# A third buffer for queries, keys and weight pieces in the attention half of an attention and mixture kernel

## The chip, the cores and the metric

The kernel runs on one core of a Trainium2 chip. The metric is the device time of one execution in microseconds (us), lower is better.

## The reference

The first half is attention over 8 batches, 8 heads, 576 positions and 64 dimensions, with a bias from a small network over relative positions. The second half is a gated feed-forward product over 4608 tokens, 512 wide, with 1024 hidden features. Cut to what matters:

```
scores = q @ k.T / sqrt(64) + bias           # bias: relu(x @ w1 + b1) @ w2, per head
attn   = exp(scores - max); attn /= sum(attn) + 1e-9
x      = (attn @ v) as [4608, 512]
h      = (x @ moe_w1) * (x @ moe_w2) @ moe_w3
out    = h @ moe_w_out
```

The four weight matrices of the second half reach the kernel as 64-bit floats and are converted to 32 bits on the chip.

## The kernel before

Attention is cut into 32 units: 4 pairs of heads (p) times 8 batches (b), with u = 8p + b. A unit has nine score tiles of 128 rows: five from head 0 and the mixed tile, the rest from head 1. For each tile TensorE multiplies queries and keys into `s` (`op_S`, L322), VectorE adds the bias and takes the row minimum of the negated scores (`op_T`, L333), ScalarE takes the exponential into `pp` (`op_E`, L362), VectorE transposes it in blocks into `pt` (`op_R`, L372), and TensorE multiplies by the values into `acc` (`op_W`, L422). ScalarE copies `acc` to `x` (`op_X`, L431 and L436), which goes to DRAM (`op_x`, L442).

Loads (`op_l`, L305) are issued on SP's queue. Keys and queries come in halves: k0, q0, k1 and q1 of a unit are four tiles of the pool `raw`, which has two buffers of each, so unit u takes the buffers of unit u-2. Values land in the lower 64 partitions only, in five parts, and GpSimd copies each part to the upper 64 (`op_V`, L310). The bias of a pair of heads is read from DRAM (`load_bias`, L284 and L275), with a small memset on GpSimd ahead of each read.

A prologue computes the bias: VectorE and ScalarE make hidden values (L532, L530), TensorE multiplies them into `bacc` (L546), ScalarE copies that to `bev` (L552, L553; eight buffers), and SP writes 36 groups to DRAM as `nb_d` (L555).

In 24 of the units, six for each pair of heads, one piece of 128 x 512 weights is converted as well. `narrow` (L163) returns its nine steps: SP fetches the 64-bit piece as `wi` (`fetch`, L176), ScalarE makes `wmag` (L181), the lower bits (L185) and the sign (L188), and GpSimd clamps (L191), doubles three times (L211) and adds and multiplies up the result (L199, L201). `wi` and `wmag` are tiles of the pool `cva`, with two buffers. The last GpSimd step of a piece (L201) is the last reader of its `wi`. GpSimd carries these steps and the copies of values in one queue.

The order of work on TensorE, VectorE, ScalarE and GpSimd is written out by hand as times within a unit's period of 12.17 us, and each of the four engines keeps it. SP's queue has planned times too (`at["c0"] = 0.2, "SP"` is the fetch of a piece in its own unit), but its order is left to the planner, which may place an issue elsewhere. An issue in SP's queue waits for its buffer to be free and for its source, and whatever stands behind it in the queue waits too.

After attention, the second half folds moe_w3 and moe_w_out into one matrix (L665 to L678) and then runs 48 steps of products (L758, L772, L828). The pieces of moe_w1 and moe_w2 are fetched by the same `narrow` into `cva` (`fetch_w`, L600).

Of the kernel before, what the change touches and what calls it, by code (L numbers as in the profile page):

```python
# [17 lines left out]
P = 128  # L18
# [104 lines left out]
def relpos_attention_moe(  # L123
# [17 lines left out]
    nc = tc.nc  # L141
# [3 lines left out]
    NTOK, DO = out.shape  # L145
# [7 lines left out]
    def f(ap):  # L153
        return ap.bitcast(F32)
# [8 lines left out]
    def narrow(pool, src, n, x, queue, pieces=1, clamps=nc.vector, signed=False):  # L163

        d = {}

        def cut(ap):
            return ap if pieces == 1 else ap.rearrange("p (c n) -> p c n", c=pieces)

        def fetch():  # L170
            if not WIDE:
                queue.dma_start(cut(x), src)
                return
            wi = pool.tile([P, n, 2], I32, name="wi")
            flat = wi.rearrange("p n t -> p (n t)")
            queue.dma_start(cut(flat), src.bitcast(I32))  # L176
            mag = pool.tile([P, n], F32, name="wmag")
            d.update(lo=wi[:, :, 0], hi=wi[:, :, 1], mag=mag, bits=mag.bitcast(I32))

        def size():  # L180
            nc.scalar.activation(d["mag"], f(d["hi"]), AF.Abs)  # L181

        def rest():

            nc.scalar.activation(x, d["lo"].bitcast(U32), AF.Copy, scale=2.0 ** -51, bias=2.0)  # L185

        def sign():
            nc.scalar.activation(f(d["hi"]), f(d["hi"]), AF.Sign)  # L188

        def clamp():  # L190
            clamps.tensor_scalar(d["mag"], d["mag"], LEAST, MOST, op0=ALU.max, op1=ALU.min)  # L191

        def shift():

            nc.vector.tensor_scalar(d["bits"], d["bits"], 3, None, op0=ALU.logical_shift_left)

        def total():

            nc.gpsimd.tensor_tensor(x.bitcast(I32), x.bitcast(I32), d["bits"], op=ALU.add)  # L199
            if not signed:  # L200
                nc.gpsimd.tensor_tensor(x, x, f(d["hi"]), op=ALU.mult)  # L201

        def mark():

            nc.vector.scalar_tensor_tensor(
                x.bitcast(I32), d["hi"], -2 ** 31, x.bitcast(I32), op0=ALU.bitwise_and, op1=ALU.bitwise_xor,
            )

        def twice():

            nc.gpsimd.tensor_tensor(d["bits"], d["bits"], d["bits"], op=ALU.add)  # L211

        steps = [fetch, size, rest, sign, clamp, shift, total]
        if signed:
            steps = [fetch, size, rest, clamp, shift, mark, total]
        if clamps is nc.gpsimd:
            steps = steps[:5] + [twice] * 3 + [total]
        return steps if WIDE else [fetch] + [lambda: None] * (len(steps) - 1)
# [17 lines left out]
    w3s = [[held.tile([P, DO], F32, name=f"w3s{t}_{hf}") for hf in range(2)] for t in range(NF)]  # L236
    wos = [held.tile([P, DO], F32, name=f"wos{t}") for t in range(NF)]
    cva = ctx.enter_context(tc.tile_pool(name="cva", bufs=2))
# [9 lines left out]


    att, att_r = ctx.enter_context(ExitStack()), ctx.enter_context(ExitStack())  # L250
    raw = att_r.enter_context(tc.tile_pool(name="raw", bufs=2, side="right"))
    nbp = att_r.enter_context(tc.tile_pool(name="nbp", bufs=2, side="right"))
    vp = []
    units = [(p, b) for p in range(NPAIR) for b in range(B)]
    NU = len(units)
# [88 lines left out]
    for i in range(2):  # L344
        t = att.enter_context(tc.tile_pool(name=f"sums{i}", bufs=1)).tile([P, 64], F32, name=f"sums{i}")
# [97 lines left out]


    def piece_of(i):
        if i < NF:
            return narrow(cva, moe_w_out[i * P:(i + 1) * P, :], DO, wos[i], nc.sync, clamps=nc.gpsimd)
        hf, t = divmod(i - NF, NF)
        return narrow(cva, moe_w3[t * P:(t + 1) * P, hf * DO:(hf + 1) * DO], DO, w3s[t][hf], nc.sync, clamps=nc.gpsimd)

    pieces = dict(zip([u for u in range(NU) if 0 < u % B < B - 1], (piece_of(i) for i in range(3 * NF))))
    assert len(pieces) == 3 * NF

# [397 lines left out]
    for i in range(2 * NF):  # L851
        hf, t = divmod(i, NF)
# [31 lines left out]
    for n in range(NPR * NF):  # L884
# [28 lines left out]
        elif 0 < p < NPR - 1 and ft in (2, 5):  # L913
            i = int(ft > 4)
# [87 lines left out]
```

## Time and profile before

| what | value |
|---|---|
| median of three runs | 1075.87 us (1073.96 to 1077.92) |
| profiled execution, span of the trace | 1078.7 us |
| TensorE matmul busy | 1044.3 us, 97% |
| VectorE busy | 778.6 us, 72% |
| ScalarE busy | 558.4 us, 52% |
| GpSimd busy | 319.4 us, 30% |
| moved by DMA | 218.36 MB, mean 202 GB/s |

The profile gives no time for its execution other than the span of the trace, which stands 0.26% above the median of the runs. TensorE's busy time counts overlapping matmuls and is not a measure of how fully it is used. VectorE's work lies mostly in the first 455 us.

### The profile page before, as it was taken

Reading aid. Unit: us, or ns where it says so; the run is one execution under the profiler, and the core shown is the slowest. Engines: PE = TensorE matmul, PEld = TensorE weight load, DVE = VectorE, ACT = ScalarE, POOL = GpSimd, SP = SyncE. Lnnn points to the kernel's source line nnn. Section 1 sums busy time; section 2 is a strip of 40 time slices with the busy share of each in tenths; the row PEclk is TensorE's granted clock in tenths of the full one; section 3 lists DMA queues with packets and bytes.
Section 4 is the critical chain, followed back from the end, with each engine's and each line's share of the span. In section 5 each row is a group of like instructions: output and inputs, shape, how many; then the busy total and the mean of one; then the engine's idle time right before and its main releaser. Section 6 shows DMA issues by size and latency. Waiting matters only on the chain.

```text
span 1078.7 us, 33624 instructions
## 1 busy us (share of the span) xinstructions
PE 1044.3 (97%) x13968; PEld 830.1 (77%) x13968; DVE 778.6 (72%) x1486; ACT 558.4 (52%) x1269; POOL 319.4 (30%) x357
## 2 busy tenths in 40 slices
PE   7989999899989999999999999999999999999998
PEld 2346666566656666678899999999999999999997
DVE  8989999899989999998888455445635544453333
ACT  6958867776867787855454322323323232332222
POOL 0057756774767488674220000000000000000000
PEclk9979999999999999999999999999999999999999
DMA  8967676766576756356856766566475566556331
GB/s 260 299 187 220 197 224 205 215 205 192 168 218 188 211 172 188 122 151 233 276 215 216 264 215 227 189 235 223 167 251 206 183 226 223 189 185 215 140 134 59
DMA packets 93593, 218.36 MB, mean 202 GB/s; under 512 B 22016, under 2 KB 46720, under 8 KB 87296
## 3 DMA queue, kind: packets, MB, share of 16 engines
q1 hardware_dynamic: 93008, 216.19, 61.1%
q8 instruction: 110, 1.80, 0.7%
q14 instruction: 43, 0.35, 0.1%
q10 hardware_dynamic: 432, 0.02, 0.0%
HBM read 171.45 MB, written 44.71 MB: 200 GB/s over the span
## 4 chain that ended last, share of the span: by engine, by line
PE 80%; DVE 9%; issue 6%; DMA 2%; ACT 2%; POOL 1%; SPq 0%; DVEq 0%; ACTq 0%; POOLq 0%
PE X L758 16%; PE acc L422 13%; PE Y L758 12%; PE s L322 12%; PE oc L828 9%; PE od L828 9%; DVE ts L333 4%; PE bacc L546 3%; DVE pt L372 3%; PE X L772 3%; PE Y L772 3%; PE wacc L678 1%; POOL w3s L667 1%; DMA wi<-in_moe_w_dram 1%; DMA w1c<-in_w_dram 0%
## 5 line engine op out<-in xcount | busy, mean ns | idle before, releaser
L422 PE MATMUL acc<-pt,v 32*64 32x160 f32 (+1 forms) x9216 | 215.9, 297 | 10.4 <-issue 10.4
L422 PEld LDWEIGHTS acc<-pt,v 32*64 32x64 f32 x9216 | 161.7, 132 | 77.5 <-issue 50.7
L362 ACT ACTIVATE pp<-ts,mx 128x576 f32<-128x576 f32 x256 | 196.0, 766 | 39.9 <-DVE mx L333 39.1
L322 PE MATMUL s<-k,q 64*128 64x288 f32 (+1 forms) x1280 | 198.4, 450 | 7.0 <-DVE mx L333 6.3
L758 PE MATMUL X<-xS,wS 128*128 128x384 f32 x960 | 194.8, 338 | 0.0
L333 DVE CUSTOM_DVE_ANT_0 ts<-s,nb 128x576 f32<-128x576 f32 x256 | 183.1, 737 | 13.5 <-PE s L322 13.2
L758 PEld LDWEIGHTS X<-xS,wS 128*128 128x128 f32 x960 | 171.5, 188 | 6.8
L372 DVE STREAM_TRANSPOSE pt<-pp 128x1152 f32<-128x1152 f32 x128 | 175.2, 1370 | 2.0 <-ACT pp L362 1.7
L322 PEld LDWEIGHTS s<-k,q 64*128 64x128 f32 (+1 forms) x1280 | 92.3, 180 | 78.9 <-issue 35.7
L758 PE MATMUL Y<-xS,wS 128*128 128x384 f32 x720 | 145.1, 336 | 0.0
L801 DVE TENSOR_TENSOR wos<-X,wos 128x384 f32<-128x384 f32 x80 | 44.6, 557 | 138.8 <-PE X L758 138.8
L310 POOL COPY v<-v 64x512 f32<-64x512 f32 (+1 forms) x160 | 87.6, 564 | 154.3 <-DMA v<-in_v_dram 141.7
L758 PEld LDWEIGHTS Y<-xS,wS 128*128 128x128 f32 x720 | 127.9, 188 | 0.1
L805 ACT COPY wos<-X 128x384 f32<-128x384 f32 x80 | 38.3, 479 | 125.6 <-PE X L758 125.6
L781 ACT ACTIVATE ghd<-wos 128x384 fp32r<-128x384 f32 x48 | 25.2, 525 | 125.7 <-DVE wos L801 105.6
L828 PE MATMUL oc<-w3s,ghc 128*128 128x512 f32 x288 | 89.8, 393 | 0.0
L828 PE MATMUL od<-w3s,ghd 128*128 128x512 f32 x288 | 89.6, 392 | 0.0
L801 DVE TENSOR_TENSOR wos<-Y,wos 128x384 f32<-128x384 f32 x80 | 44.6, 557 | 49.9 <-ACT wos L805 36.4
L211 POOL TENSOR_TENSOR wmag<-wmag 128x512 int32<-128x512 int32 x72 | 74.7, 1038 | 5.9
L781 ACT ACTIVATE ghc<-wos 128x384 fp32r<-128x384 f32 x48 | 25.2, 526 | 93.8 <-DVE wos L801 76.2
L828 PEld LDWEIGHTS oc<-w3s,ghc 128*128 128x128 f32 x288 | 53.5, 188 | 8.6
L828 PEld LDWEIGHTS od<-w3s,ghd 128*128 128x128 f32 x288 | 53.5, 188 | 8.5
(97 smaller groups left out, 1401.5 us busy)
## 6 DMA issues: line engine op xcount, KB each, us to landing
wS<-w_d SPq DMA_DIRECT2D x40, 1792.0 KB, 7.4
q<-in_q_dram SPq DMA_DIRECT2D x64, 288.0 KB, 4.3
wi<-in_moe_w_dram SPq DMA_DIRECT2D x32, 512.0 KB, 3.9
w_d<-wS SPq DMA_DIRECT2D x8, 1792.0 KB, 6.6
v<-in_v_dram SPq DMA_DIRECT2D x96, 128.0 KB, 4.4
nb_d<-bev SPq DMA_DIRECT2D x36, 295.5 KB, 4.2
k<-in_k_dram SPq DMA_DIRECT2D x64, 144.0 KB, 4.4
nb<-nb_d SPq DMA_DIRECT2D x16, 576.0 KB, 5.5
```

What stands on the lines that cost most here:

```text
L211: nc.gpsimd.tensor_tensor(d["bits"], d["bits"], d["bits"], op=ALU.add)
L310: nc.gpsimd.tensor_copy(t[64:128], t[0:64])
L322: nc.tensor.matmul(s[outs, hf, :HS], d[f"q{h}"][rows, q0:q0 + n], d[f"k{h}"][rows, :], start=True, stop=True,)
L333: nc.vector.tensor_tensor_reduce(out=halves(ts), in0=d.pop(("s", t))[:, :, :HS], in1=halves(NB[p, t]), op0=ALU.add, op1=ALU.min, scale=-1. ...
L362: nc.scalar.activation(d["p", ps][:, k * S:(k + 1) * S], ts, AF.Exp, bias=mx, scale=-1.0, accum_out=SUMS[u // 4 % 2][:, col:col + 1],)
L372: nc.vector.transpose(o, st[u].pop(("p", ts)))
L422: nc.tensor.matmul(acc[outs, a, c0:c0 + 32 * (t1 - t0)], d["v", b][rows, h], pt_[rows, t0:t1, 32 * b:32 * b + 32], start=(b == 0), stop=(b ...
L758: nc.tensor.matmul(acc, w[:, l, W_AT[n], i * P:(i + 1) * P], x[:, r, X_AT[n]], start=(k in "125" and i == 0 and m == 0), stop=(i == 1 and ...
L772: nc.tensor.matmul(acc, w[:, l, i * P:(i + 1) * P], x[:, r, 2 * k + "cd".index(j)], start=(n == 0), stop=(n == 11),)
L781: nc.scalar.activation(st[n], st["g" + j], AF.Copy)
L801: nc.vector.tensor_tensor(st[o], x, y, op=op)
L828: nc.tensor.matmul(d["o", j, t], l[:, sl], folded[ft][r], start=(ft == 0 and n == 0), stop=(ft == NF - 1 and n == 2),)
```

## The change

The pool `raw` gets a third buffer of each of its four tiles, so a unit takes the buffers of the unit three before. A new pool `cvb` with one buffer holds `wi` and `wmag` of every third weight piece; the other two of three stay in `cva`. So a piece takes the buffers of the piece three before. No instruction is added or taken away, and the planned times stay. The new pool and the larger one lie in on-chip memory until the end of attention.

```
-    raw = att_r.enter_context(tc.tile_pool(name="raw", bufs=2, side="right"))
+    raw = att_r.enter_context(tc.tile_pool(name="raw", bufs=3, side="right"))
     nbp = att_r.enter_context(tc.tile_pool(name="nbp", bufs=2, side="right"))
+    cvb = att_r.enter_context(tc.tile_pool(name="cvb", bufs=1, side="right"))
...
     def piece_of(i):
+        cv = cvb if i % 3 == 2 else cva
         if i < NF:
-            return narrow(cva, moe_w_out[i * P:(i + 1) * P, :], DO, wos[i], nc.sync, clamps=nc.gpsimd)
+            return narrow(cv, moe_w_out[i * P:(i + 1) * P, :], DO, wos[i], nc.sync, clamps=nc.gpsimd)
         hf, t = divmod(i - NF, NF)
-        return narrow(cva, moe_w3[t * P:(t + 1) * P, hf * DO:(hf + 1) * DO], DO, w3s[t][hf], nc.sync, clamps=nc.gpsimd)
+        return narrow(cv, moe_w3[t * P:(t + 1) * P, hf * DO:(hf + 1) * DO], DO, w3s[t][hf], nc.sync, clamps=nc.gpsimd)
```

## Rows read from the trace of the kernel before

**Rows 1.** Windows: us, busy (x instructions) by engine, TensorE clock, DMA share, GB/s.
```profile
150.00:200.00 50.00, 49.55 (x1380) 32.09 (x1364) 49.53 (x98) 38.47 (x95) 30.71 (x41) 1.00 0.68 202
200.00:250.00 50.00, 45.72 (x1211) 29.96 (x1215) 45.22 (x89) 35.79 (x88) 38.99 (x45) 0.97 0.73 213
...
300.00:350.00 50.00, 45.46 (x1180) 29.69 (x1180) 43.76 (x86) 34.65 (x87) 34.14 (x41) 0.93 0.69 200
```

**Rows 2.** Timeline of TensorE in one stall: start, us, work, idle before.
```profile
320.11 0.69 PE L422 MATMUL acc<-pt,v 32*64 32x160 f32 x2 [3.11 <-issue]
```

**Rows 3.** Timeline of GpSimd around the same stall.
```profile
308.07 1.30 POOL L201 TENSOR_TENSOR w3s<-w3s,wi 128x512 f32<-128x512 f32 x1
...
318.88 0.60 POOL L310 COPY v<-v 64x512 f32<-64x512 f32 x1 [5.57 <-DMA v<-in_v_dram]
```

**Rows 4.** Timeline of SP's queue around the same stall.
```profile
309.39 0.33 SPq L176 DMA_DIRECT2D wi<-in_moe_w_dram  x1
...
314.20 0.51 SPq L305 DMA_DIRECT2D v<-in_v_dram  x1
```

**Rows 5.** Waits of SP's queue, 50 to 430 us: total, times, longest.
```profile
SPq L176 <- POOL w3s L201: 50.0, 12, 6.0
SPq L305 <- PE s L322: 33.6, 72, 1.6
```

**Rows 6.** Tile k: the matmuls' idle time by what ended it: us, times.
```profile
  DVE mx L333: 36.8, 91
  issue: 35.7, 132
```

**Rows 7.** Tile wi: its readers, and their idle time that its transfer ended.
```profile
L181 ACT ACTIVATE wmag<-wi x40: 643/670/688, 68.9 to 566.2; 128x512 f32<-128x512 f32 x40
...
  DMA wi<-in_moe_w_dram: 2.3, 2
```

**Rows 8.** Timeline of SP's queue in the prologue.
```profile
7.34 0.43 SPq L176 DMA_DIRECT2D wi<-in_moe_w_out_dram  x1
10.32 2.40 SPq L555 DMA_DIRECT2D nb_d<-bev  x2
12.77 0.59 SPq L176 DMA_DIRECT2D wi<-in_moe_w_out_dram  x1
```

**Rows 9.** DMA issues: KB each, median us from issue to landing.
```profile
q<-in_q_dram SPq DMA_DIRECT2D x64, 288.0 KB, 4.3
wi<-in_moe_w_dram SPq DMA_DIRECT2D x32, 512.0 KB, 3.9
...
k<-in_k_dram SPq DMA_DIRECT2D x64, 144.0 KB, 4.4
```

**Rows 10.** Windows of the prologue and behind it, columns as in rows 1.
```profile
0.00:5.00 5.00, 0.00 (x0) 0.00 (x0) 0.40 (x1) 1.28 (x1) 0.44 (x6) 1.00 0.56 156
0.00:20.00 20.00, 12.79 (x112) 5.55 (x112) 15.36 (x40) 11.68 (x24) 0.44 (x6) 1.00 0.80 252
20.00:50.00 30.00, 28.29 (x230) 8.78 (x226) 30.00 (x89) 28.14 (x64) 0.00 (x0) 1.00 0.94 303
60.00:65.00 5.00, 4.68 (x20) 1.95 (x20) 4.05 (x10) 3.36 (x8) 2.01 (x4) 0.50 0.50 141
```

**Rows 11.** Timeline of SP's queue where the bias is last written and read.
```profile
54.00 0.53 SPq L555 DMA_DIRECT2D nb_d<-bev  x1
...
60.46 0.45 SPq L275 DMA_DIRECT2D nbM<-nb_d  x1
```

**Rows 12.** Tile bev: issue to landing of its writes, min, median, max.
```profile
DMA to landing us min/median/max: 3.2/4.2/6.9
```

**Rows 13.** Timeline at the end of attention.
```profile
447.26 0.39 SPq L176 DMA_DIRECT2D wi<-in_moe_w_dram  x1
...
452.30 1.06 POOL L310 COPY v<-v 64x512 f32<-64x512 f32 x2 [3.40 <-DMA v<-in_v_dram]
...
453.00 2.48 PE L422 MATMUL acc<-pt,v 32*64 32x160 f32 x112
```

## The prediction

> **What bounds the kernel now.** I read the windows first, since the page's shares mix two halves with different limits. In an undisturbed stretch of attention VectorE is busy for 49.53 of 50 us, so there VectorE sets the pace. Two stretches fall short of it: 45.22 us in 200 to 250 and 43.76 in 300 to 350 [rows 1]. Taking the undisturbed stretch as the level, they lose 49.53 - 45.22 = 4.31 and 49.53 - 43.76 = 5.77 us, together 10.1 us. That is the prize in this part of the kernel, and whatever the new buffers may save has to be found there, at the start, or at the end of attention. The second half of the kernel touches none of the new tiles.
>
> The timelines show what such a stall is made of. TensorE stands idle 3.11 us before a value product at 320.11 [rows 2]. The product needed a part of the values that GpSimd had copied at 318.88, and GpSimd had stood idle 5.57 us for its transfer [rows 3]. That transfer was issued only at 314.20, in a queue where SP had been held until 309.39 by the fetch of a weight piece [rows 4]. The fetch waited for GpSimd's last step on an older piece, which ended at 308.07 + 1.30 = 309.37 [rows 3]. So a late GpSimd holds SP, SP sends the values late, and late values make GpSimd later. SP's waits on that step come to 50.0 us in 12 waits between 50 and 430 us, and its waits for the score product that frees keys and queries to 33.6 us in 72 [rows 5]. These waits are what the change is aimed at.
>
> The next question is whether the loads that get a third buffer are themselves ever late. They are not. The score products, which read keys and queries, stood idle chiefly for VectorE's row minimum (36.8 us, it frees the score buffers) and for issue (35.7 us), with no transfer of keys or queries at the head of the list [rows 6]. The readers of the weight pieces waited 2.3 us in all for the pieces' transfers [rows 7]. What is late is the values, and they get no new buffer.
>
> **The change part by part.**
>
> No instruction is added or removed on any engine, so no engine gets more or less work. What can change is when SP's issues go out.
>
> *Where the planner puts a load.* Here lies the choice on which the forecast rests. If SP kept its planned times, a fetch with three buffers would find its buffer free a period earlier, and the waits in rows 5 would go. But SP does not keep them. The fetches of pieces 0 and 1 are planned in units 1 and 2, behind every write of the bias, and they stand in the queue at 7.34 and at 12.77, among the first of those writes [rows 8], while the first reader of a piece runs at 68.9 [rows 7]. They are placed as soon as a buffer is free by the planner's reckoning, however early that is. The fetch at 309.39 is the same case: it is issued 0.02 us after the step that frees its buffer, and it stands ahead of value loads that are planned before it. With a third buffer the planner does the same with one buffer more. At the start it fills three sets instead of two. From then on, the load that stands behind the release of a given buffer is the one for the unit three ahead instead of two ahead, at the same place in the queue and with the same wait on the same instruction. The data come a period earlier, which no reader needed, and the values stand behind the same waits as before.
>
> *Weight pieces in the steady state.* The wait of each fetch on L201 stays, 50.0 us of SP's time in rows 5, and so do the two stalls: 0 us. From the other side, if all of those waits went and took the stalls along, 10.1 us would be gained.
>
> *Keys and queries in the steady state.* Same place, same wait for the score product: 0 us. They are covered by the distance between load and use, a whole unit; a loss would need them later than now, and nothing makes them later.
>
> *The start.* The third set is loaded in the prologue: two halves of keys, two of queries and a weight piece, 2 x 144 + 2 x 288 + 512 = 1376 KB, or 1.41 MB [rows 9]. At 303 GB/s, the rate of 20 to 50 us [rows 10], that is 4.65 us of transfer. It is free if it fits in the gaps. The DMA engines are busy 0.80 of the first 20 us and 0.94 of the next 30, which leaves 4.0 + 1.8 = 5.8 us; but 0.44 x 5 = 2.2 us of it lie in the first 5 us, before these loads can be sent, so 3.6 us are left [rows 10]. 4.65 - 3.6 = 1.05 us would still be ahead of the last bias data at 50 us. That matters there, because SP waits from 54.00 until 60.46 for the last bias write to land before it can read the mixed tile's bias, and loads of values stand behind that read [rows 11]. I take 1.0 us. The lower bound is 0 (the landing is hidden by the prologue's compute, in which VectorE is busy for all of 20 to 50 us) and the upper 4.65 (no gap can be used). The issues themselves, five at some 0.4 to 0.6 us as in rows 8, are covered by the eight buffers of `bev`: a write may be late until its buffer is wanted again eight groups on, the 36 writes go out from 10.32 to 54.00 [rows 8, 11], 1.25 us apart, so eight take 10 us, and the writes land in 4.2 us at the median and 6.9 at most [rows 12]. If that cover is gone, they cost up to 3 us, within the upper bound above.
>
> *The end.* The second half's first two fetches take buffers of `cva`. The last piece now sits in `cvb`, so they move up one place in the queue and one place falls empty: the one at 447.26, where a fetch holds SP until GpSimd is done with the last piece. The values behind it go earlier, and GpSimd's 3.40 us of idle time at 452.30 can shrink. TensorE takes up its value products at 453.00, before the second of those copies is done at 453.36 [rows 13], so these copies release nothing that TensorE was held for. I take 0; the bound is a gain of 3.4 us.
>
> The sum: +1.0 at the start, 0 in the steady state, 0 at the end. On the profiled execution 1078.7 + 1.0 = 1079.7 us; on the median of the runs, 2.8 us below it, 1075.87 + 1.0 = 1076.9 us. The bounds of these terms alone give 1075.9 - 3.4 = 1072.5 to 1075.9 + 4.65 = 1080.5.
>
> **The rivals.**
>
> *The waits go, and it is faster.* If the planner leaves the fetches near their planned places, or finds the free buffer but puts values ahead of them, SP is no longer held by GpSimd and the loop of lateness is broken. For it speaks that the stalls begin exactly there [rows 3, 4]; against it, the place of the fetches in rows 8 and of the one in rows 4. The time is 1075.9 - 10.1 = 1065.8 us if both stalls go, and 1075.9 - 5.8 = 1070.1 if one does. The Trainium skill (Perfetto Trace Analysis, Optimization Strategy) says that a gap which keeps coming back on the engine that ought to be saturated can mean that too few buffers are there for the next tile. By that rule the kernel would gain these 10.1 us; the trace agrees that a buffer's release is waited for, but shows the tile behind that wait, the values, to be another than the ones that get buffers.
>
> *The start is bound by its transfers, and it is slower.* If none of the 4.65 us fits in a gap, the last bias write lands so much later than 60.46, and the values behind it too. TensorE is already slowed then: from 60 to 65 us its granted clock is 0.50, the lower of its two levels, and VectorE is busy for 4.05 of 5 us [rows 10]. TensorE would stand idle longer before, and if the slow stretch grows by the same 4.65 us, VectorE loses another 0.95 / 5 of it, 0.9 us, up to all of it. That is 4.65 + 0.9 = 5.6 to 9.3 us, so 1081.5 to 1085.2. It decides from 5.4 us on. Against it stand the gaps in the shares, and that ScalarE and VectorE bound the prologue.
>
> *The change does nothing at all* is the forecast itself but for 1.0 us.
>
> **How the numbers follow.** About 0.5%, 5.4 us, is what a measurement of this kernel can tell from no change. The forecast, with the order of the queue moving up along with the buffers, gets 0.64, and all of its own range, 1072 to 1081, lies within 0.5%. The faster rival gets 0.18: rows 8 speak plainly, but only of the start. The slower one gets 0.18, less likely in its full size, but the only part of the sum that is sure to exist is at the start. So faster 0.18, same 0.64, slower 0.18. The range has to take in most of both rivals to leave out no more than 2 in 10: from 1066, where both stalls go, to 1083, the lower half of the slow case.
>
> **What would show it.** Right: three fetches of weight pieces and three sets of keys and queries in SP's queue before 30 us; SP's waits on L201 of the w3 pieces still near 50 us between 50 and 430; VectorE short of its pace again near 206 to 222 and 309 to 325 us; the first score tiles later by about 1 us. Wrong: the waits on L201 gone and no shortfall of VectorE in those windows (the first rival); the last bias write landing 4 us later or `bev` waiting for its buffers (the second). The forecast fails altogether if the planner's new order moves the value loads themselves, since one stall more or less is worth 4 to 6 us.

## The result: slower by 0.7%, lost at the hand-over from the bias to attention

The changed kernel takes 1083.38 us (median of 6 runs, 1078.79 to 1084.35) where the kernel before takes 1075.91 in the same session: ratio 1.0068, 95% interval [1.0042, 1.0094]. The forecast was 1076.9 with a range of 1066 to 1083, so the time lies just above the range, on the side that had a chance of 0.18.

The windows of the kernel after, first those that answer to [rows 1], with the same columns:

```profile
150.00:200.00 50.00, 48.94 (x1322) 31.77 (x1316) 49.02 (x96) 36.68 (x92) 31.17 (x39) 1.00 0.72 204
200.00:250.00 50.00, 46.89 (x1282) 30.69 (x1285) 47.31 (x94) 37.73 (x93) 36.19 (x42) 1.00 0.68 200
...
300.00:350.00 50.00, 47.26 (x1258) 30.68 (x1259) 46.87 (x94) 37.37 (x92) 36.51 (x43) 0.99 0.69 204
...
20.00:50.00 30.00, 28.30 (x230) 8.84 (x228) 30.00 (x89) 28.09 (x65) 0.00 (x0) 1.00 0.97 327
50.00:100.00 50.00, 39.45 (x739) 22.88 (x745) 38.37 (x75) 29.61 (x71) 22.11 (x27) 0.80 0.66 200
55.00:60.00 5.00, 0.13 (x2) 0.00 (x0) 0.00 (x0) 0.39 (x2) 0.00 (x0) 0.89 0.94 326
60.00:65.00 5.00, 2.29 (x8) 1.15 (x8) 4.40 (x7) 1.63 (x4) 2.62 (x5) 0.50 0.57 159
...
70.00:75.00 5.00, 3.99 (x18) 2.03 (x16) 4.95 (x9) 2.78 (x7) 0.00 (x0) 0.50 0.59 178
75.00:80.00 5.00, 5.00 (x80) 2.62 (x78) 3.17 (x6) 2.48 (x7) 3.76 (x4) 0.56 0.07 14
```

Of the kernel before, the same view of the stretches that the prediction had not shown:

```profile
50.00:100.00 50.00, 44.97 (x926) 26.59 (x928) 44.65 (x88) 35.57 (x85) 26.98 (x33) 0.86 0.67 201
...
70.00:75.00 5.00, 5.00 (x140) 3.20 (x124) 3.49 (x8) 2.47 (x7) 4.71 (x5) 0.69 0.30 87
75.00:80.00 5.00, 5.00 (x167) 3.29 (x157) 3.53 (x9) 3.68 (x9) 3.93 (x6) 1.00 0.58 173
```

From 55 to 60 us the computing engines all but stand still while the DMA engines are 0.94 busy. VectorE does 44.65 - 38.37 = 6.28 us less of its work between 50 and 100 us. After the pause TensorE's granted clock is 0.50, the lower of its two levels, up to 75 us and 0.56 up to 80; before it was 0.69 from 70 us and back at 1.00 from 75 us on. The prologue itself is not later: from 20 to 50 us the engines are as busy as in [rows 10], and only the transfers are more, 327 GB/s where there were 303. The two stalls of [rows 1] are still there, in other sizes.

What stands still is visible on VectorE. Its timeline after, and then before:

```profile
54.24 0.08 DVE L334 DVE_READ_ACCUMULATOR2_ANT mx<- 128x1 f32 x1
60.60 1.38 DVE L373 STREAM_TRANSPOSE pt<-pp 128x1152 f32<-128x1152 f32 x1 [6.28 <-DMA v<-in_v_dram]
```

```profile
54.34 1.37 DVE L372 STREAM_TRANSPOSE pt<-pp 128x1152 f32<-128x1152 f32 x1
```

The first transpose of attention starts at 60.60 instead of 54.34 and waits 6.28 us for a DMA. It reads and writes nothing that a transfer brings. The name in the brackets is only that of the transfer that landed last. SP's timeline after says which one it is:

```profile
53.90 0.53 SPq L557 DMA_DIRECT2D nb_d<-bev  x1
...
60.17 0.45 SPq L276 DMA_DIRECT2D nbM<-nb_d  x1
```

The last write of the bias is issued at 53.90 (before: 54.00 [rows 11]), and SP's read that needs all of them to have landed goes out at 60.17. The transpose follows 0.43 us later. Before, only SP waited for that landing, now VectorE does too, and with it TensorE:

```profile
62.69 2.29 PE L323 MATMUL s<-k,q 64*128 64x288 f32 x8 [7.56 <-DVE mx L334]
```

**Why it waits: where the tiles lie.** The bigger pools sit on the right side of on-chip memory, ahead of the prologue's pool of `bev`. A third set of keys and queries takes 2 x 1152 + 2 x 2304 = 6912 B in each partition (144 and 288 KB over 128 partitions, [rows 9]), a third `wi` and `wmag` 4096 + 2048 = 6144 B, together 13,056 B. That moves the eight `bev` buffers (2368 B each) down. In the memory map of the built kernel before they start 3040 B above the end of `pt`, the transposes' output. No trace shows that map, but the first experiment finds the border between 3040 and 3072 B. After the change 13,056 - 3040 = 10,016 B are common to both. So the first transpose may not write until the transfers out of `bev` are done.

The queue did what was forecast. SP's waits after, 50 to 430 us, which answer to [rows 5]:

```profile
SPq L176 <- POOL w3s L201: 45.4, 13, 6.1
...
SPq L306 <- PE s L323: 26.1, 46, 3.7
```

The fetches still wait for the same step, 45.4 us in 13 waits where there were 50.0 in 12, and the loads for the score products that free keys and queries, 26.1 us in 46 where there were 33.6 in 72. The profiled executions are closer than the medians: 1081.8 against 1078.7 us is +3.1. VectorE lost 6.28 us between 50 and 100 us, and between 100 and 450 us (sum of the seven windows) it did 339.99 us against 336.80, 3.19 more, because this execution's later stalls were smaller: 6.28 - 3.19 = 3.09. That the two figures meet so closely is chance. Between the medians lie 7.5 us. That the later stalls even out over many executions and only the start remains is a reading, since there is one trace of each kernel; the first experiment's 7.0 us agree with it.

### The profile page after: what moved, and what is told of

The parts are those of the page before. It is cut to its first block, busy times and chain, and to the rows that moved or that the text cites. A ratio compares the mean times of both kernels' runs of the same rounds, so it can differ in the third digit from the quotient of the medians.

```text
span 1081.8 us, 33616 instructions
## 1 busy us (share of the span) xinstructions
PE 1043.5 (96%) x13968; PEld 829.8 (77%) x13968; DVE 780.3 (72%) x1486; ACT 558.5 (52%) x1269; POOL 319.2 (30%) x357
## 4 chain that ended last, share of the span: by engine, by line
PE 83%; DVE 6%; issue 4%; DMA 2%; ACT 2%; POOL 2%; SPq 0%; DVEq 0%; ACTq 0%; POOLq 0%
PE X L760 16%; PE acc L423 15%; PE s L323 14%; PE Y L760 12%; PE oc L830 9%; PE od L830 9%; PE bacc L548 3%; PE X L774 3%; PE Y L774 3%; DVE ts L334 3%; DVE pt L373 2%; POOL w3s L669 1%; DMA wi<-in_moe_w_dram 1%; DMA v<-in_v_dram 0%; ACT bev L555 0%
```

## Experiments

The theory to test was memory (the place of `bev` against `pt`); its rivals were the extra loads in the prologue and the new order of the queue. Further down come the two later stalls, on which the prediction rested.

**A dead pool in the kernel before, 3040 B and 3072 B.** No load, buffer or queue changes, but for one small memset on GpSimd.

```
     nbp = att_r.enter_context(tc.tile_pool(name="nbp", bufs=2, side="right"))
+    gap = att_r.enter_context(tc.tile_pool(name="gap", bufs=1, side="right")).tile([P, 760], F32, name="gap")
+    nc.gpsimd.memset(gap[:, 0:8], 0.0)
```

The second has 768 columns in place of 760.

> The kernel before with 3040 bytes per partition of dead space between the bias tiles and the prologue's eight bev buffers, so that bev ends up exactly against pt without sharing a byte with it. It loads nothing more and has no third buffer. Memory theory (the larger pools push bev into the place of pt, and the first transpose waits for the last bias write to land): no shared byte, so no stall at the first transpose and a time within 2 us of before. Transfer theory (the third set's loads in the prologue delay it): no more loads, within 2 us of before too. It is the control of the next run.

> The same with 3072 bytes, 32 more, so that bev and pt share 32 bytes per partition. Still no third buffer and no more loads. Memory theory: the first transpose waits from about 54.4 until the last bias write lands at about 60.4 us, VectorE stands idle some 6 us there, and the run is 5 to 8 us slower than before (ratio 1.005 to 1.007). Transfer theory and queue theory (the third buffers change the order of SP's queue): as in the control, within 2 us of before.

Measured: 1075.74 us, ratio 1.0009 [0.9996, 1.0021], and 1082.78 us, ratio 1.0060 [1.0035, 1.0086]. VectorE's timeline with 3040 B and with 3072 B, and SP's with 3072 B:

```profile
54.40 1.37 DVE L374 STREAM_TRANSPOSE pt<-pp 128x1152 f32<-128x1152 f32 x1
```

```profile
59.76 1.38 DVE L374 STREAM_TRANSPOSE pt<-pp 128x1152 f32<-128x1152 f32 x1 [5.18 <-DMA v<-in_v_dram]
```

```profile
54.15 0.52 SPq L557 DMA_DIRECT2D nb_d<-bev  x1
...
59.70 0.45 SPq L277 DMA_DIRECT2D nbM<-nb_d  x1
```

32 B of unused memory cost 7.0 us between the two medians. The transpose starts 0.06 us after the read that waits for the last write. The loss of the change is there without any of its buffers or loads.

**The change, and the kernel before, with the two pools apart.** In both the pool `pt` is opened ahead of the values' pools, so that it lies elsewhere, and `bev` has seven buffers.

```
-        ep = pro.enter_context(tc.tile_pool(name="ep", bufs=8, side="right"))
+        ep = pro.enter_context(tc.tile_pool(name="ep", bufs=7, side="right"))
...
-    vp += [att.enter_context(tc.tile_pool(name=f"vp{i}", bufs=1)) for i in range(2)]
     pt = att.enter_context(tc.tile_pool(name="pt", bufs=1))
+    vp += [att.enter_context(tc.tile_pool(name=f"vp{i}", bufs=1)) for i in range(2)]
```

> The changed kernel with pt placed below the value pools instead of above them and seven bev buffers instead of eight, so that pt and bev share nothing (the second unit's values do). All third buffers and the loads of the third set in the prologue stay. Memory theory: no stall at the first transpose, and 5 to 8 us faster than the changed kernel, so within 3 us of before. Transfer theory: the extra 1.41 MB are still loaded, so it stays 5 to 8 us slower than before. Queue theory: the order of SP's queue is that of the changed kernel, so it stays slower too.

> The kernel before with the same two placements as the run with pt and bev apart (pt below the value pools, seven bev buffers), and two buffers as before. All theories: within 2 us of before. What the run with third buffers differs from this one by is the worth of the buffers and their loads: 0 to +1.5 us by the memory theory, 5 to 8 us by the transfer theory.

Measured: with third buffers 1073.36 us, ratio 0.9990 [0.9972, 1.0009]; with two, 1073.63, ratio 0.9990 [0.9975, 1.0005]. The first transpose of the one with third buffers:

```profile
54.25 1.37 DVE L373 STREAM_TRANSPOSE pt<-pp 128x1152 f32<-128x1152 f32 x1
```

The stall is gone with all the loads in place. What the third buffers do besides, in the queue, at the start and at the end, is the difference of these two: -0.3 us, nothing that can be told from zero with intervals of some 2 us to either side.

**One half of the change each.** First only `raw` with three buffers, then only `cvb` with `raw` at two.

```
-    raw = att_r.enter_context(tc.tile_pool(name="raw", bufs=2, side="right"))
+    raw = att_r.enter_context(tc.tile_pool(name="raw", bufs=3, side="right"))
```

> One half of the change: three buffers of keys and queries, weight pieces as before. The pool is 6912 bytes larger, so bev's first two buffers reach into pt. Memory theory: any shared byte brings the whole wait, so the first transpose starts at about 60 us and the run is 5 to 8 us slower than before, as with 32 shared bytes. A theory by amounts (the cost grows with the shared bytes or with the bytes loaded) would give about half, 3 to 4 us.

> The other half: every third weight piece in tiles of its own, two buffers of keys and queries. The pool of 6144 bytes also moves bev's first two buffers into pt. Memory theory: the same whole wait, 5 to 8 us slower than before. Theory by amounts: 3 to 4 us.

Measured: 1082.84 us, ratio 1.0070 [1.0043, 1.0097], and 1085.61 (4 runs), ratio 1.0097 [1.0069, 1.0124]. VectorE's timeline of the second:

```profile
60.45 1.38 DVE L373 STREAM_TRANSPOSE pt<-pp 128x1152 f32<-128x1152 f32 x1 [6.07 <-DMA nb_d<-bev]
```

6912 - 3040 = 3872 B and 6144 - 3040 = 3104 B in common are enough for all of the loss, as the 32 B were. The parts do not add up, the price is that of one wait. Here the wait is even named after the write of `bev`. The second costs 0.3% more than the whole change and more than the 5 to 8 us expected; the intervals overlap. Its trace has a stall that belongs to neither theory, TensorE waiting for queries:

```profile
245.20 1.33 PE L323 MATMUL s<-k,q 64*128 64x288 f32 x4 [2.60 <-DMA q<-in_q_dram]
```

Whether the other three executions have it too is open.

**SP freed from the fetches, then from every wait for GpSimd.** The prediction held that late GpSimd work keeps SP, and SP the values [rows 2 to 4]. First the pieces of attention are fetched from ScalarE's queue, in the kernel before and in the change with the pools apart; then the small memsets of `load_bias` move to VectorE as well.

```
-            return narrow(cva, moe_w_out[i * P:(i + 1) * P, :], DO, wos[i], nc.sync, clamps=nc.gpsimd)
+            return narrow(cva, moe_w_out[i * P:(i + 1) * P, :], DO, wos[i], nc.scalar, clamps=nc.gpsimd)
...
-            nc.gpsimd.memset(nb[:, 0, 0:1], 0.0)
+            nc.vector.memset(nb[:, 0, 0:1], 0.0)
```

> The kernel before, with the weight pieces of attention fetched from ScalarE's queue instead of SP's, so that the fetch stands at its planned place in ScalarE's order and SP never waits for GpSimd's last step on a piece. Two buffers as before, nothing moved in memory. Theory that SP is held by those fetches and so sends the values late: SP's waits on L201 in 50 to 430 us, 50 to 70 us in all, are gone, VectorE is busy for over 48 of 50 us in 200 to 250 and 300 to 350, and the run is 4 to 10 us faster than before (ratio 0.991 to 0.996). Rival (the values are held by the bias reads and their memset on GpSimd, or by GpSimd itself): within 2 us of before, and the two windows stay near 45 us.

> The same fetches from ScalarE's queue, in the changed kernel with pt and bev apart. The fetch now stands at a planned place and does not move up with the buffers, so the third buffer of the pieces is real slack. If the release of the piece's buffer is still waited for in ScalarE's queue with two buffers, this is faster than the run before it by up to 3 us; if not, the same within 1.5 us.

> The run with weight pieces fetched from ScalarE's queue, and in addition the 15 small memsets ahead of the bias reads on VectorE instead of GpSimd, so that SP's queue waits for GpSimd neither before a fetch nor before a bias read. Two buffers, memory as before. Theory that the values are late because SP is held by a late GpSimd, whichever instruction it waits on: the 63.9 us and 9.2 us of SP's waits on the memsets go too, VectorE is busy for over 48 of 50 us in 200 to 250 and 300 to 350, and it is 4 to 8 us faster than the run before it in this line (1076.9), less some 1.5 us of memsets on VectorE. Rival (GpSimd's own queue is what delays the copies of values: their conversions stand ahead of them, whenever SP sends them): within 2 us of that run, and the two windows stay below 47 us.

> The same with the third buffers of keys, queries and pieces, and with pt and bev apart. First theory: as the run above, or up to 2 us faster where a third buffer takes away a wait for a score product or for a piece's last step. Rival: within 2 us of the run with three buffers and ScalarE's queue (1076.6).

Measured, as ratios: fetches moved, 1.0020 [1.0008, 1.0033] (1076.86 us) and, with third buffers, 1.0005 [0.9982, 1.0028]; memsets moved too, 1.0009 [0.9988, 1.0031] (1074.84 us) and 0.9994 [0.9973, 1.0014]. SP's waits with the fetches moved, and with both moved and two buffers:

```profile
SPq L305 <- PE acc L422: 67.8, 74, 3.5
SPq L284 <- POOL nb L281: 63.9, 12, 8.3
```

```profile
SPq L305 <- PE acc L422: 130.6, 109, 4.2
...
SPq L284 <- DVE nb L281: 6.7, 7, 1.3
```

The windows of the last one:

```profile
200.00:250.00 50.00, 46.65 (x1213) 30.78 (x1206) 44.32 (x89) 35.22 (x86) 37.47 (x42) 0.93 0.66 201
300.00:350.00 50.00, 48.18 (x1310) 31.44 (x1308) 47.28 (x99) 37.93 (x94) 40.35 (x46) 0.97 0.69 213
```

With two buffers the waits on L201 are gone, then all longer waits for GpSimd, and VectorE still has 44.32 us in 200 to 250, less than the 45.22 of [rows 1]; in 300 to 350 it has 47.28, more than the 43.76 there. TensorE's longest gap in the first of these windows:

```profile
235.12 1.33 PE L422 MATMUL acc<-pt,v 32*64 32x128 f32 x20 [2.19 <-issue]
```

An SP that GpSimd holds is not what makes the stalls. SP still waits in these runs, now for TensorE (130.6 us), so that values could be late for another reason; the gaps themselves decide that.

**What TensorE waits for instead.** In the kernel before it has five gaps of more than 0.7 us in attention's steady state. They are put down to "issue", and they lie in the middle of a value product, which reads one `pt` and one part of the values: in three of them 62 or 63 of its 64 matmuls have already run, in the one of [rows 2] 46 of 48 and in the one at 236.20 us 44 of 64. No new value can be missing there. In 200 to 250 us they come to 1.41 + 2.01 + 0.86 = 4.28 us, where VectorE falls short by 4.31. Two of them, beside the one in [rows 2]:

```profile
215.16 0.43 PE L422 MATMUL acc<-pt,v 32*64 32x160 f32 x2 [2.01 <-issue]
...
307.73 0.29 PE L422 MATMUL acc<-pt,v 32*64 32x160 f32 x1 [0.99 <-issue]
```

Windows that run from the start into these three gaps count what TensorE has done by then:

```profile
0.00:214.50 214.50, 196.68 (x4282) 112.52 (x4283) 202.47 (x437) 163.73 (x388) 106.08 (x133) 0.97 0.75 226
0.00:307.30 307.30, 286.84 (x6703) 171.27 (x6704) 291.06 (x610) 232.58 (x558) 168.03 (x207) 0.97 0.73 217
...
0.00:318.50 318.50, 296.10 (x6958) 177.19 (x6959) 302.02 (x630) 239.56 (x574) 173.69 (x213) 0.97 0.73 216
```

6958 - 6703 = 255 matmuls, with their weight loads 510 instructions. The page of the profile lists a DMA queue of instructions:

```profile
q8 instruction: 110, 1.80, 0.7%
```

That is 110 packets of 16.4 KB. TensorE's 2 x 13,968 = 27,936 matmuls and loads and 185 semaphore and drain instructions of its sequencer, which the trace also holds, are 28,121, one packet for every 256 (28,121 / 256 = 109.8). Counted with the sequencer's, the five gaps begin after 8385, 8641, 9665, 13,505 and 14,017 instructions: 1, 4, 15 and 2 times 256 apart. In the other traces, too, every gap of over 0.7 us in the middle of a value product lies on this grid, to within one instruction. Theory A is that TensorE ran out of instructions. The DMA view of 316.0 to 317.4, and of 317.5 to 318.7, in the gap that ends at 320.11:

```profile
q1 hardware_dynamic: 363, 0.34, 94.8%
```

```profile
q1 hardware_dynamic: 129, 0.11, 33.1%
q8 instruction: 1, 0.02, 6.2%
```

Data take 94.8% of the 16 DMA engines until 317.4. The instruction packet runs only after that, and TensorE goes on 1.4 us behind its end. In all five gaps the packet before it ends 1.3 to 1.5 us before TensorE goes on.

**TensorE's program moved by 64 instructions.** If blocks of instructions are late, the gaps stay at the same count and move in the work; if a value or a semaphore is late, they stay at the same work.

```
         acc = psb.tile([P, 1024], F32, name="bacc")
+        if G == 0:
+            for _ in range(16):
+                nc.tensor.matmul(acc[0:GM, 0:8], w2b, zs[0][:, 0:8], start=True, stop=True)
```

> The kernel before, with 16 matmuls of 8 columns and their 16 weight loads put ahead of the first group of the bias, so that all later work of TensorE stands 32 instructions further on in its program. Theory A (blocks of instructions come late): the gaps in the middle of a value product begin 32 instructions, that is 16 matmuls, earlier in the work: where the kernel before has 1 or 2 matmuls of a part left after the gap (208.17, 215.16, 307.73, 320.11) there are 17 or 18 left, and where it has 20 left (236.20) there are 36. Theory B (a semaphore, values that come late): the work that has to wait is the same, so 1, 2 and 20 are left as before. The time is within 2 us of the kernel before by both.

Measured: 1075.97 us, ratio 1.0006 [0.9987, 1.0025]. Each of these f32 products runs as two matmuls (x14000 against x13968 in all), so the shift is 32 matmuls and 32 loads, twice what the expectation counted. Two of the gaps, and the windows that run into them:

```profile
216.76 0.97 PE L422 MATMUL acc<-pt,v 32*64 32x160 f32 x34 [0.70 <-issue]
...
306.53 0.83 PE L422 MATMUL acc<-pt,v 32*64 32x160 f32 x33 [1.00 <-issue]
```

```profile
0.00:216.40 216.40, 196.05 (x4282) 111.23 (x4283) 202.11 (x435) 162.59 (x386) 106.28 (x133) 0.96 0.73 224
0.00:306.20 306.20, 284.52 (x6703) 168.89 (x6704) 290.81 (x607) 232.31 (x558) 168.18 (x207) 0.97 0.72 217
```

The counts are the same, 4282 and 6703, to the matmul. The work is not: 34 and 33 matmuls of the part are left where 2 and 1 were, 32 more in both. Theory A holds. Not every block is late: 4155, 4792 and 6958 show no such gap in this execution, and others do.

**An eighth of each weight piece.** Fewer bytes, same instructions and waits in the steady state.

```
-            wi = pool.tile([P, n, 2], I32, name="wi")
-            flat = wi.rearrange("p n t -> p (n t)")
-            queue.dma_start(cut(flat), src.bitcast(I32))
+            if clamps is nc.gpsimd:
+                wi = FIXED[len(TAKEN) % 2]
+                TAKEN.append(1)
+                flat = wi.rearrange("p n t -> p (n t)")
+                queue.dma_start(flat[:, 0:128], src.bitcast(I32)[:, 0:128])
```

> The kernel before, with two fixed tiles for attention's weight pieces, of which only the first 128 of 1024 columns are fetched: it leaves out seven eighths of the transfer of each of the 24 pieces (448 of 512 KB, 10.8 MB in all), every instruction of TensorE, VectorE, ScalarE and GpSimd and every wait of the steady state stays. Theory A (TensorE is held in the middle of a value product because its next block of instructions comes late while the DMA engines are saturated by a 512 KB piece): the gaps of over 0.7 us in the middle of a value product, of which the kernel before has five and which cost up to 3.11 us, shrink or vanish, VectorE is busy for over 48 of 50 us in 200 to 250 and in 300 to 350, and the time is 4 to 8 us below the kernel before. Theory B (TensorE waits for values that come late because GpSimd holds SP's queue): GpSimd has the same work and SP the same waits for it, so both stalls stay, VectorE is busy for 44 to 46 of 50 us there, and the time is within 2 us of the kernel before.

Measured: 1065.23 us, ratio 0.9908 [0.9885, 0.9931], 9.9 us below the kernel before by the ratio, more than theory A's 4 to 8. Windows, the page's row of the value products (with that of the kernel before ahead of it), and SP's waits:

```profile
200.00:250.00 50.00, 49.25 (x1316) 31.77 (x1314) 49.12 (x96) 38.59 (x94) 38.16 (x45) 1.00 0.66 187
...
300.00:350.00 50.00, 49.15 (x1318) 31.41 (x1315) 49.52 (x96) 38.60 (x96) 36.88 (x44) 1.00 0.66 189
```

```profile
L422 PE MATMUL acc<-pt,v 32*64 32x160 f32 (+1 forms) x9216 | 215.9, 297 | 10.4 <-issue 10.4
```

```profile
L433 PE MATMUL acc<-pt,v 32*64 32x128 f32 (+1 forms) x9216 | 214.0, 295 | 1.9 <-issue 1.8
```

```profile
SPq L178 <- POOL w3s L207: 41.5, 13, 5.7
...
SPq L178 <- POOL wos L207: 19.5, 6, 6.0
```

No gap of over 0.7 us is left in the middle of a value product, the value products' idle time falls from 10.4 to 1.9 us, VectorE is above 49 of 50 us in both stretches, and SP is held by GpSimd as often as ever. TensorE's idle stretches of over 0.3 us between 85 and 450 us come to 10.1 us in the trace of the kernel before, 9.7 of them on the grid of 256; all the kernels that load every byte have 4.7 to 9.7 us on the grid, and this one has 1.4. The stalls come from the bytes, not from the waits. This kernel leaves out 448 KB of each of 24 pieces and is no version to use. None of the versions that do all the work is clearly faster than the kernel before.

## Why the prediction was wrong

**The step that failed is the one that is not in it.** "No instruction is added or removed on any engine" was right, but "what can change is when SP's issues go out" was not all: buffers also take room. The prediction looked at loads, waits and queues and never at which tiles share memory. That was one sum away: 13,056 B of growth against 3040 B of room. The missing term is about +7 us, and the dead pool alone gave 7.0. At the start it had set +1.0 with an upper bound of 4.65 for loads alone, so no bound held the new wait. Its first transpose waited 6.28 us instead.

**The queue, 0 us: right.** SP's order behind the prologue is the old one, with each of these loads for a unit or a piece further on. Waits on L201 stay (45.4 us in 13). The view in [rows 6] adds the idle time of the weight loads to that of the matmuls, so its 36.8 and 35.7 us are not what the score products waited; for them the page has 7.0 us:

```profile
L322 PE MATMUL s<-k,q 64*128 64x288 f32 (+1 forms) x1280 | 198.4, 450 | 7.0 <-DVE mx L333 6.3
```

That no load of keys or queries is at the head of the list stays true. Keys and queries, and the end of attention, cost and give nothing: the difference of the two kernels with pools apart is -0.3 us for all of it together, inside the bounds of 0 to +4.65 and 0 to -3.4.

**The start, +1.0 us: the loads cost nothing.** The last bias write went out at 53.90 against 54.00, and the read behind its landing at 60.17 against 60.46. Two forecasts of what the profile would show missed. The first score tiles were to come about 1 us later, and VectorE's first work on one starts at 50.60 against 50.70. And three fetches of pieces were to go out before 30 us. SP's timeline after:

```profile
17.61 0.76 SPq L176 DMA_DIRECT2D wi<-in_moe_w_out_dram  x1
...
47.74 0.58 SPq L176 DMA_DIRECT2D wi<-in_moe_w_out_dram  x1
...
65.78 0.58 SPq L176 DMA_DIRECT2D wi<-in_moe_w_out_dram  x1
```

Only the first does; the second goes out at 47.74 (before: 12.77 [rows 8]) and the third at 65.78. So the planner did not fill a buffer as soon as it was free, and the prologue carried only the keys and queries of the third set, 864 KB and not the 1376 KB of the sum. That these cost nothing that can be measured is shown; that a third piece would cost nothing there is not.

**The slower rival: right in sign and size, wrong in cause.** It asked for the bias to land 4.65 us later. The landing did not move, a second engine was put behind it. So it is luck that 1083.38 lies within its 1081.5 to 1085.2. Its other half held: behind the longer pause TensorE stood at the lower clock for longer (0.50 up to 75 us, where before it was 0.69 from 70 us on).

**The faster rival: falls twice.** The waits did not go. And when other edits took them away, the 10.1 us were not there, since the stalls are late instructions. The reading of [rows 2 to 4] as a chain from GpSimd to SP to the values was the second error of the prediction: the product at 320.11 had only 2 matmuls left to run, so the copy that ended at 318.88 + 0.60 us was not what it lacked. It did no harm to the number, because the change left those waits where they were. The rule of the Trainium skill (Perfetto Trace Analysis, Optimization Strategy), that a recurring gap on the engine that ought to be saturated can mean too few buffers, does not fit this gap: a third set gave -0.3 us.

## What to carry to other kernels

A larger pool is a move of every pool behind it: before adding buffers, compare the growth with the room up to the next tiles that live a little later, above all where a stage that ends in transfers hands its memory to the next. When the first instruction on a new tile waits for a transfer that it does not need, look for the tile that had its place. And a gap that the profile calls "issue", in the middle of a run of equal matmuls, is not a late tile: count the instructions up to it before blaming a queue.

## What the runs showed of the hardware

TensorE's instructions come by DMA and compete with data. Here a block of 256 instructions came late up to six times in an execution and cost 0.7 to 3.1 us each, always at a count of the program on the same grid of 256; which blocks are late differs from one execution to the next. With 448 of 512 KB left out of 24 transfers, 9.9 us came back. The Trainium skill (Runtime: NRT & Kernel Launch, Instruction fetch mechanics) says that the sequencer fetches blocks of 16 KiB, 256 instructions, through a DMA queue of its own, and that the cost of going from one block to the next is mostly hidden. The trace agrees on the size (1.80 MB in 110 packets); most blocks do pass without a gap of that size, but the late ones are not hidden. The packets of the five late blocks took no longer than others (1.2 to 1.6 us, all of them 0.9 to 1.7 between 85 and 450 us), but began late: 2.6 to 5.1 us after TensorE had entered the block before, where the median of the other 69 in that stretch is 1.2 us. What stays open is why only some blocks are late: whether the request goes out late or its packet queues behind the data was not separated.
